# Attention inside a feed-forward kernel: products with v moved directly behind the scores, into another PSUM bank

## The chip, the cores and the metric

One core of a Trainium2 chip. The metric is the device time of one execution in microseconds, the median of the runs. TensorE is called PE here, VectorE DVE, ScalarE ACT, GpSimd POOL and SyncE SP.

## The reference

Windowed attention with eight memory keys for each head, followed by an RMS norm and a gated feed-forward layer, all in float32:

```python
for c in range(S // 32):                       # S = 768, chunks of 32 queries
    k_full = concat([mem_k, k[c0 - 16:c1 + 8]])  # 8 memory keys, 16 left, 32 own, 8 right
    a = softmax(q_c @ k_full.T / 8)
    out_c = a @ v_full
x = out as (4 * 768, 8 * 64)                   # tokens by heads * head_dim = 512
xn = x / sqrt(mean(x * x) + 1e-6) * rms_g
y = (silu(xn @ w_gate) * (xn @ w_val)) @ w_out  # d_ff = 1536
```

## The kernel before

**Blocks.** The 3072 tokens are eight blocks of 384. The feed-forward layer walks over them. Blocks 0 and 1 come first, in an order written out by hand (ORDER). Then come the segments of blocks 0, 2 and 3: for each of up to twelve slices f of d_ff, `moe_in` computes the gate `pg` (12 matmuls of 384 columns, three for each product because each float32 operand is held as a high and a low part), a second `moe_in` the value `pv` (12 more), and `moe_out` (L529) adds the product of the slice before into `po` (9 matmuls of 512 columns). Blocks 4 to 7 come last, two at a time, with products of combined operands (`whole`, `products`, L1001, and `out_products`, L1084).

**Late attention.** The attention of blocks 2 to 7 is not computed ahead: it is cut into steps, and a generator, `late_steps`, yields after each. It works on pairs of head units; n counts the pairs. One turn of the generator takes the pair `old`, whose softmax is done, through these steps: 'p' transposes the softmax of both units on PE (`stage_p`, L282, six transposes into two banks) and lets ACT copy them out (`stage_c`, L286, recorded at L181); 's' computes the scores of the next pair `cur` (`stage_s2`, L219), their maxima and differences on DVE and the exponentials on ACT (L247); 'o' multiplies the copies with v (`stage_o2`, L313), copies the result into x (`late_r`, L324), squares it on ACT (L327) and adds the squares on DVE (L329). After every second pair the norm follows: `late_n` splits the sum of squares and adds it over the partitions on PE (`ssum`, L341).

`stage_o2` writes the even chunks (`oe`) and the odd ones (`oo`) into two PSUM banks. `oe` takes one of the three rotating banks, and `oo`, where `own` is false (blocks 2 to 5), the bank of tag "v", which `pv` uses:

```python
stage_o2(old, None if own else "v")
```

The first unit's transposes use the gate's bank in these turns (`stage_p(u, None if i or own else "g")`). Each of these banks has a single buffer, so a new user waits for the last reader of the one before.

**Where the steps stand.** A table, VISITS, says which steps run in which gap of which segment. Gap 2n lies behind the gate of the n-th slice, 2n + 1 behind its value, and 2n + 1.5 behind the `moe_out` that follows. At 5: 'ps', 5.5: 'o' the transposes and scores run behind the value, then come the nine matmuls of `moe_out`, then the products with v, then the next slice's gate. The steps for blocks 6 and 7 (n from 9 on, `own` true) stand in a second table, SUPER, between the products of `whole(2)`.

**What sets the order.** From the segments on, PE runs in the order of the program (`on_pe`). The order on DVE, ACT, POOL and SP is made by a planner that goes by priorities; `tc.high_priority()` puts steps ahead, and `tc.issue_after(i)` puts an instruction behind another on its engine. Between the visits, DVE and ACT also compute sums of weights for the last blocks (`keep`, L838 to L851, and `sums_o`, L866 to L875), in amounts that tables give for each gap; each is issued behind the last DVE and ACT instructions traced so far. At n = 9 the step 'o' runs behind product 10 of the second pair of `whole(2)`; the add that takes a bank's result there (`add`, L977) is what frees the bank for the next product that uses it.

Of the kernel before, what the change touches and what calls it, by code (L numbers as in the profile page):

```python
# [14 lines left out]
ALU = mybir.AluOpType  # L15
# [24 lines left out]
YMAX = 0x1DFE / 0x1000 * 2.0 ** -96  # L40


VISITS = {0: {1: 's', 5: 'ps', 5.5: 'o', 7: 'ps', 7.5: 'o', 9: 'n', 10: 'n', 11: 'n'}, 2: {5: 'ps', 5.5: 'o', 17: 'ps', 17.5: 'o', 19: 'n', 20: 'nn'}, 3: {3: 'ps', 3.5: 'o', 7: 'ps', 7.5: 'o', 9: 'n', 9.5: 'n', 10: 'n', 11: 'ps', 11.5: 'o', 15: 'ps', 15.5: 'o', 17.5: 'n', 18: 'n', 19: 'n'}}
PAIRS = ((1, 2), (3, 4), (5, 6), (7, 8), (0, 9), (10, 11))
NR = 30

# [40 lines left out]
def tile_kernel(ctx: ExitStack, tc: tile.TileContext, q, k, v, w_gate, w_val, w_out, rms_g, out, out_t):  # L87
    nc = tc.nc
# [6 lines left out]
    ps = {"a": ps_cm.enter_context(tc.tile_pool(name="psa", bufs=3, space=PSUM))}  # L95
# [30 lines left out]
    def on_pe(ins):  # L126
        if pinned:
            tc.keep_in_program_order(ins)

    def psum_a(name):  # L130
        return ps["a"].tile([P, 512], F32, name=name, tag="at")

    def psum_m(tag, name):
        return psm.tile([P, 512], F32, name=name, tag=tag)
# [7 lines left out]
    late, late_cm = {}, {}  # L142
# [13 lines left out]
    def load_qk(u):  # L156
        d = st.setdefault(u, {})
        if u < NE:
            d["q"] = early.tile([P, HT], F32, name=f"q{u}", tag=f"q{u % 6}")
            t = early.tile([P, KN], F32, name=f"k{u}", tag=f"k{u % 6}")  # L160
            nc.sync.dma_start(out=d["q"], in_=q[u])
        else:

            t = late["kv", u % 2][:, 0:KN]
            d["q"] = late["q", u % 2]
            nc.sync.dma_start(out=d["q"], in_=q[u])
        d["k"] = t.rearrange("p (j k) -> p j k", j=NJ)
        nc.sync.dma_start(out=t, in_=k[u])

    def load_v(u):  # L170
        t = early.tile([P, VN], F32, name=f"vw{u}", tag=f"v{u % 6}") if u < NE else late["kv", u % 2][:, KN:]
        st.setdefault(u, {})["v"] = t.rearrange("p (j h d) -> p j h d", j=NJ, h=2)
        nc.sync.dma_start(out=t, in_=v[u])
# [33 lines left out]
    def stage_s2(pair):  # L207

        for u in pair:
            st[u]["s"] = psum_a(f"s{u}")  # L210
        for i in range(NT):
            for cp in range(2):
                for par in range(2):
                    c, o = 4 * i + 2 * par + cp, (2 * i + cp) * KC
                    for u in pair:
                        d = st[u]
                        for e in range(2):
                            r, a = slice(64 * e, 64 * e + 64), 64 * par + CH * (e ^ u % 2)
                            on_pe(nc.tensor.matmul(d["s"][a:a + CH, o:o + KC], lhsT=d["q"][r, c * CH:c * CH + CH],  # L219
                                                   rhs=d["k"][r, c // 2, 40 * cp:40 * cp + KC], start=True, stop=True))  # L220

    def stage_m(u):
        stage_ma(u)
        stage_mb(u)
# [20 lines left out]
    def stage_e(u):  # L245
        pe = st[u]["p"]
        nc.scalar.activation(pe, pe, AF.Exp, scale=0.125)  # L247

    def stage_d(u):
        stage_da(u)  # L250
        stage_db(u)
# [25 lines left out]
    def stage_p(u, tag=None):  # L277
        d = st[u]
        t = psum_m(tag, f"pT{u}") if tag else psum_a(f"pT{u}")
        pe = d["p"].rearrange("p j k -> p (j k)")  # L280
        for i in range(NT):
            on_pe(nc.tensor.transpose(out=t[:, i * P:(i + 1) * P], in_=pe[:, i * P:(i + 1) * P], identity=ident))  # L282
        d["t"] = t

    def stage_c(u):
        copy("a", late["pt", u % 2], st[u]["t"][:, 0:HT])  # L286
# [17 lines left out]
    def stage_o2(pair, tag):  # L304

        st["o2"] = o2 = [psum_a(f"oe{pair[0]}"), psum_m(tag, f"oo{pair[0]}") if tag else psum_a(f"oo{pair[0]}")]
        for j in range(NJ):
            for n, u in enumerate(pair):
                pt = late["pt", u % 2].rearrange("p (j e q) -> p j e q", j=NJ, e=2)
                for cp in range(2):  # L310
                    r, o = slice(64 * cp, 64 * cp + 64), (NJ * n + j) * CH
                    for hh in range(2):
                        on_pe(nc.tensor.matmul(o2[cp][64 * hh:64 * hh + 64, o:o + CH], lhsT=st[u]["v"][r, j, hh],  # L313
                                               rhs=pt[r, j, hh ^ u % 2], start=True, stop=True))

    def late_r(pair, x):

        g = units[pair[0]][2]
        o2 = st["o2"]
        for u in pair:  # L320
            st.pop(u)
        xc = x[g // 2].rearrange("p g (j c q) -> p g j c q", c=2, q=CH)
        for cp in (1, 0):
            nc.scalar.copy(xc[:, :, :, cp], o2[cp][:, 0:HT].rearrange("p (g j q) -> p g j q", g=2, q=CH))  # L324
        for i in range(g, g + 2):
            s = obuf(f"sq{i}")[:, 0:HT]
            nc.scalar.activation(s, x[i // 2][:, i % 2], AF.Square)  # L327
            if i:
                nc.vector.tensor_tensor(out=s, in0=s, in1=late["ss"], op=ALU.add)  # L329
            late["ss"] = s  # L330

    def late_n(x, parts=1):

# [198 lines left out]
    def obuf(name):  # L532
        return p3.tile([P, DM], F32, name=name, tag="stg")
# [30 lines left out]
    def last_of(eng):  # L564
        return next(i for i in reversed(nc.cur_bb.bb.instructions) if i.engine == eng.engine)
# [3 lines left out]
    def late_steps():  # L569


        pairs = [(u, u + 1) for u in range(NE, len(units), 2)]
        for n in range(len(pairs) + 1):
            old = pairs[n - 1] if n else ()
            cur = pairs[n] if n < len(pairs) else ()
            new = pairs[n + 1] if n + 1 < len(pairs) else ()
            own = bool(old) and old[0] >= 3 * 2 * NG
            if old and old[0] % NG == 0:
                if old[0] // NG in (5, 7):
                    late_x["x"] = [p1.tile([P, 2, HT], F32, name="x1", tag="wy"),  # L580
                                   late["tmp"][:, 0:2 * HT].rearrange("p (g t) -> p g t", g=2)]
                else:
                    t = p1.tile([P, NKT, HT], F32, name="xT", tag="x")
                    late_x["x"] = [t[:, 0:2], t[:, 2:4]]
                late_x[old[0] // NG] = late_x["x"]
            x = late_x.get("x")
            if old:
                with tc.high_priority():
                    for i, u in enumerate(old):
                        stage_p(u, None if i or own else "g")  # L590
                    for u in old:
                        stage_c(u)
                yield "p"
            if cur:
                with tc.high_priority():
                    stage_s2(cur)
                    for u in cur:
                        stage_m(u)
                    for u in cur:
                        stage_e(u)  # L600
            for u in new:
                load_qk(u)
            if old:
                if cur:
                    yield "s"
                with tc.high_priority():
                    stage_o2(old, None if own else "v")
                    late_r(old, x)
            norm = late_n(x, 1 if cur else 2) if n and n % 2 == 0 else ()
            behind = ExitStack()  # L610
            if norm:
                with tc.high_priority():
                    next(norm)
                behind.enter_context(tc.issue_after(last_of(nc.vector)))
            if own and norm and cur:
                for u in cur:
                    load_v(u)
                yield "o"
                next(norm)
                yield "n"  # L620
                with tc.high_priority():
                    for u in cur:
                        stage_d(u)
                yield "d"
            else:
                with tc.high_priority(), behind:
                    for u in cur:
                        stage_d(u)
                for u in cur if n else ():
                    load_v(u)  # L630
                yield "o" if old else "s"
            for _ in norm:
                yield "n"
# [79 lines left out]
    def tok_o(n):  # L713
# [15 lines left out]
        g=tok_in("g"), v=tok_in("v"), p=tok_q("g"), q=tok_q("v"),  # L729
# [427 lines left out]
    for blk, fs in segments:  # L1157
# [3 lines left out]
        def visit(gap):  # L1161
# [3 lines left out]
            sums_out()  # L1165
            for c in VISITS[blk].get(gap, ""):
                if next(todo) != c:
                    raise AssertionError(gap)
            keep(SUMS_AT[blk].get(gap, 0), summing)
        for n, f in enumerate(fs):  # L1170
            g = moe_in("g", f, xs)
# [132 lines left out]
```

## Time and profile before

| | us |
|---|---|
| median of 3 runs (652.34 to 655.0) | 652.45 |
| the profiled execution | 652.04 |
| its span, first to last instruction | 650.2 |
| PE busy | 638.2 |
| DVE busy | 489.4 |
| ACT busy | 366.2 |

The profile is of one execution. Busy time of PE counts each matmul from its start to a modelled end, and neighbours overlap, so that the distance from one start to the next is what a matmul costs in a run of them.

### The profile page before, as it was taken

How to read it: one execution, taken by the hardware profiler on the slowest of the kernel's cores; microseconds unless marked ns; L12 is line 12 of the kernel's file. 1: busy time of each engine (PE TensorE's matmuls, PEld its weight loads, DVE VectorE, ACT ScalarE, POOL GpSimd, SP SyncE). 2: the span in 40 equal slices, each digit the busy share in tenths (PEclk: the TensorE clock that was granted, in tenths of full speed). 3: DMA queues.
4: the chain of work that ended last, by engine and by line, in shares of the span. 5: the costliest groups of instructions: out<-in, count | busy, mean ns of one | idle time of the engine just before them, and what ended most of it. 6: DMA issues, size and time to landing. Idle time of an engine off the chain costs nothing.

```text
span 650.2 us, 15459 instructions
## 1 busy us (share of the span) xinstructions
PE 638.2 (98%) x6110; PEld 603.9 (93%) x6110; DVE 489.4 (75%) x999; ACT 366.2 (56%) x691; POOL 13.8 (2%) x19
## 2 busy tenths in 40 slices
PE   6999999999999999999999999999999999999997
PEld 4789999999899999999999999999999999999997
DVE  6999899768698888876888865567679854544864
ACT  4998877744545546465565454555566443333463
POOL 0200000000000000000000000000000000000000
PEclk7999999999999999999999999999999999999999
DMA  8737544269797887265459998887878988887711
GB/s 322 295 131 258 191 162 162 111 221 322 222 383 284 302 303 266 79 208 204 134 168 368 356 314 289 268 285 223 264 224 275 302 275 253 255 252 253 251 36 73
DMA packets 94006, 155.14 MB, mean 239 GB/s; under 512 B 8048, under 2 KB 47344, under 8 KB 93936
## 3 DMA queue, kind: packets, MB, share of 16 engines
q1 hardware_dynamic: 91920, 150.93, 69.2%
q10 hardware_dynamic: 2016, 3.25, 1.4%
q8 instruction: 48, 0.79, 0.5%
q14 instruction: 22, 0.18, 0.1%
HBM read 114.03 MB, written 40.11 MB: 237 GB/s over the span
## 4 chain that ended last, share of the span: by engine, by line
PE 94%; DMA 2%; ACT 2%; DVE 1%; issue 0%; SPq 0%
PE po L529 16%; PE pg L473 16%; PE pv L473 15%; PE mga L1001 8%; PE pa L1084 8%; PE mva L1001 8%; PE pe L1084 4%; PE mge L1001 4%; PE mve L1001 4%; PE oe L313 2%; PE s L219 2%; PE pc L1084 2%; PE mvc L1001 2%; PE mgc L1001 2%; PE pT L282 1%; DMA ws<-in_moe_w_val_dram 1%
## 5 line engine op out<-in xcount | busy, mean ns | idle before, releaser
L473 PE MATMUL pg<-xh,wh_g 128*128 128x384 f32 x192 | 65.9, 343 | 0.0
L473 PE MATMUL pv<-xh,wh_v 128*128 128x384 f32 x192 | 64.9, 338 | 0.5 <-ACT xT L324 0.5
L473 PE MATMUL pg<-xh,wl_g 128*128 128x384 f32 x192 | 64.6, 337 | 0.0
L473 PE MATMUL pg<-xl,wh_g 128*128 128x384 f32 x192 | 64.6, 336 | 0.0
L473 PE MATMUL pv<-xh,wl_v 128*128 128x384 f32 x192 | 64.3, 335 | 0.0
L473 PE MATMUL pv<-xl,wh_v 128*128 128x384 f32 x192 | 64.2, 334 | 0.0
L1001 PE MATMUL mga<-x,r 128*128 128x384 f32 x288 | 58.0, 335 | 0.0
L1001 PE MATMUL mva<-x,r 128*128 128x384 f32 x288 | 57.7, 334 | 0.0
L529 PE MATMUL po<-wh_o,hh 128*128 128x512 f32 x141 | 55.9, 396 | 0.0
L529 PE MATMUL po<-wl_o,hh 128*128 128x512 f32 x141 | 55.6, 394 | 0.0
L529 PE MATMUL po<-wh_o,hl 128*128 128x512 f32 x141 | 55.6, 394 | 0.0
L1052 ACT CAST hho<-h 128x384 fp32r<-128x384 f32 x72 | 37.0, 514 | 32.7 <-PE pa L1084 19.0
L1001 PEld LDWEIGHTS mva<-x,r 128*128 128x128 f32 x288 | 50.6, 188 | 0.0
L1001 PEld LDWEIGHTS mga<-x,r 128*128 128x128 f32 x288 | 50.5, 188 | 0.1
L1084 PE MATMUL pa<-hho,r 128*128 128x384 f32 x192 | 50.3, 335 | 0.0
L1053 DVE TENSOR_TENSOR hlo<-h,hho 128x384 fp32r<-128x384 f32 x72 | 39.3, 555 | 13.3 <-ACT hho L1052 12.4
L181 ACT CAST hh<-t 128x384 fp32r<-128x384 f32 x45 | 23.2, 516 | 44.1 <-PE po L529 20.3
L473 PEld LDWEIGHTS pg<-xh,wh_g 128*128 128x128 f32 x192 | 36.1, 188 | 1.8
L473 PEld LDWEIGHTS pv<-xh,wh_v 128*128 128x128 f32 x192 | 36.0, 188 | 1.7 <-ACT xT L324 0.9
L473 PEld LDWEIGHTS pg<-xl,wh_g 128*128 128x128 f32 x192 | 36.1, 188 | 1.4 <-DVE xl L676 0.2
L473 PEld LDWEIGHTS pv<-xl,wh_v 128*128 128x128 f32 x192 | 36.0, 188 | 0.3
L473 PEld LDWEIGHTS pg<-xh,wl_g 128*128 128x128 f32 x192 | 36.0, 188 | 0.0
(195 smaller groups left out, 1561.3 us busy)
## 6 DMA issues: line engine op xcount, KB each, us to landing
r<-kg SPq DMA_DIRECT2D x84, 256.0 KB, 3.8
r<-kv SPq DMA_DIRECT2D x84, 256.0 KB, 3.6
r<-ko SPq DMA_DIRECT2D x84, 256.0 KB, 3.2
kv<-in_v_dram SPq DMA_DIRECT2D x24, 384.0 KB, 4.4
kv<-in_k_dram SPq DMA_DIRECT2D x24, 312.0 KB, 4.4
q<-in_q_dram SPq DMA_DIRECT2D x20, 192.0 KB, 4.2
ws<-in_moe_w_gate_dram SPq DMA_DIRECT2D x6, 512.0 KB, 3.7
ws<-in_moe_w_val_dram SPq DMA_DIRECT2D x6, 512.0 KB, 4.6
```

The costliest lines, as they stand in the source:

```text
L181: return nc.scalar.copy(out, in_)
L219: on_pe(nc.tensor.matmul(d["s"][a:a + CH, o:o + KC], lhsT=d["q"][r, c * CH:c * CH + CH], rhs=d["k"][r, c // 2, 40 * cp:40 * cp + KC], star ...
L282: on_pe(nc.tensor.transpose(out=t[:, i * P:(i + 1) * P], in_=pe[:, i * P:(i + 1) * P], identity=ident))
L313: on_pe(nc.tensor.matmul(o2[cp][64 * hh:64 * hh + 64, o:o + CH], lhsT=st[u]["v"][r, j, hh], rhs=pt[r, j, hh ^ u % 2], start=True, stop=True))
L473: on_pe(nc.tensor.matmul(ps[:, 0:HT], lhsT=weight(a, n, f, kt), rhs=xs[c][:, kt], start=kt == first and i == 0, stop=kt == last and i == 2))
L529: on_pe(nc.tensor.matmul(po[i], lhsT=h[a][:, i * P:(i + 1) * P], rhs=weight(c, "o", f), start=f == first and n == 0, stop=f == end and n = ...
L1001: on_pe(nc.tensor.matmul(bank[w, b], lhsT=r[:, a, kt], rhs=x[:, c, kt], start=bool(first) and kt == 0 and i == 0, stop=kt == 1 and i == 2, ...
L1052: nc.scalar.copy(hh, x)
L1053: nc.vector.tensor_tensor(out=hl, in0=x, in1=hh.bitcast(F32), op=ALU.subtract)
L1084: on_pe(nc.tensor.matmul(bank[c][i], lhsT=w[u][:, x, i * P:(i + 1) * P], rhs=uhl[u][y], start=p == 0 and n == 0 and m in (1, 2, 5), stop=p ...
```

## The change

The eight visits in blocks 0, 2 and 3 run 'pso' in one gap, behind the value and ahead of `moe_out`; the gaps 2n + 1.5 are empty after it. In these turns the odd products go into the bank of tag "g". For the odd n with `own` true (9 and 11), the second add of squares is not issued in `late_r`: it is held and issued at the start of the next turn, ahead of its transposes.

```diff
-VISITS = {0: {1: 's', 5: 'ps', 5.5: 'o', 7: 'ps', 7.5: 'o', 9: 'n', ...
+VISITS = {0: {1: 's', 5: 'pso', 7: 'pso', 9: 'n', ...
...
-    def late_r(pair, x):
+    def late_add(s):
+        nc.vector.tensor_tensor(out=s, in0=s, in1=late["ss"], op=ALU.add)
+        late["ss"] = s
+
+    def late_r(pair, x, hold=False):
...
             nc.scalar.activation(s, x[i // 2][:, i % 2], AF.Square)
-            if i:
-                nc.vector.tensor_tensor(out=s, in0=s, in1=late["ss"], op=ALU.add)
-            late["ss"] = s
+            if not i:
+                late["ss"] = s
+            elif hold:
+                late["held"] = s
+            else:
+                late_add(s)
...
             if old:
                 with tc.high_priority():
+                    if "held" in late:
+                        late_add(late.pop("held"))
                     for i, u in enumerate(old):
                         stage_p(u, None if i or own else "g")
...
-                    stage_o2(old, None if own else "v")
-                    late_r(old, x)
+                    stage_o2(old, None if own else "g")
+                    late_r(old, x, own and n % 2 == 1)
```

In segment 2 the gaps 5 and 17 are changed in this way, in segment 3 the gaps 3, 7, 11 and 15.

## Rows read from the trace of the kernel before

**Rows 1.** Page: busy time and instructions by engine, and the chain that ended last.

```profile
PE 638.2 (98%) x6110; PEld 603.9 (93%) x6110; DVE 489.4 (75%) x999; ACT 366.2 (56%) x691; POOL 13.8 (2%) x19
...
PE 94%; DMA 2%; ACT 2%; DVE 1%; issue 0%; SPq 0%
```

**Rows 2.** Busy time by stretch: bounds, us, then each engine, granted clock, DMA.

```profile
150.00:328.00 178.00, 177.32 (x2184) 163.20 (x2183) 147.36 (x331) 94.67 (x193) 2.43 (x2) 1.00 0.72 244
```

**Rows 3.** PE's timeline in one visit: start, us, line, tiles, shape, count.

```profile
169.89 0.23 PE L219 MATMUL s<-kv,qp 64*32 64x64 f32 x2
170.05 0.50 PE L529 MATMUL po<-wh_o,hh 128*128 128x512 f32 x1
...
171.31 0.39 PE L529 MATMUL po<-wh_o,hl 128*128 128x512 f32 x1
...
171.99 0.39 PE L529 MATMUL po<-wh_o,hl 128*128 128x512 f32 x1
172.31 0.25 PE L313 MATMUL oe<-pt,kv 64*64 64x32 f32 x2
...
173.69 0.23 PE L313 MATMUL oo<-kv,kv 64*64 64x32 f32 x2
173.84 0.45 PE L473 MATMUL pg<-xh,wh_g 128*128 128x384 f32 x1
174.13 0.34 PE L473 MATMUL pg<-xl,wh_g 128*128 128x384 f32 x1
174.30 0.35 PE L473 MATMUL pg<-xh,wl_g 128*128 128x384 f32 x1
```

**Rows 4.** PE's timeline after the visit at 157 us; idle time and releaser in brackets.

```profile
165.14 0.34 PE L473 MATMUL pg<-xh,wl_g 128*128 128x384 f32 x1
166.01 0.44 PE L473 MATMUL pv<-xh,wh_v 128*128 128x384 f32 x1 [0.53 <-ACT xT L324]
166.29 0.34 PE L473 MATMUL pv<-xl,wh_v 128*128 128x384 f32 x1
```

**Rows 5.** ACT's timeline, same stretch.

```profile
165.49 0.47 ACT L324 COPY xT<-oo 128x384 f32<-128x384 f32 x1
```

**Rows 6.** PE's timeline in `whole(2)`, behind the step 'o' of n = 9.

```profile
399.83 1.20 PE L1001 MATMUL mva<-x,r 128*128 128x384 f32 x6
401.72 1.32 PE L1001 MATMUL mve<-x,r 128*128 128x384 f32 x6 [0.69 <-DVE e L977]
```

**Rows 7.** DVE's timeline, same stretch.

```profile
400.64 0.56 DVE L329 TENSOR_TENSOR sq<-sq,sq 128x384 f32<-128x384 f32 x1 [2.83 <-ACT sq L327]
401.12 0.55 DVE L977 TENSOR_TENSOR e<-mve,e 128x384 f32<-128x384 f32 x1
```

**Rows 8.** PE's timeline at the norm's column sums.

```profile
261.01 0.34 PE L341 MATMUL ssum<-sh,one 128*128 128x384 f32 x1
261.49 0.44 PE L341 MATMUL ssum<-sl,one 128*128 128x384 f32 x1
```

**Rows 9.** ACT's timeline in the visit of rows 3.

```profile
169.10 0.49 ACT L181 COPY kv<-pT 128x384 f32<-128x384 f32 x1
171.64 0.53 ACT L247 ACTIVATE pe<-pe 128x384 f32<-128x384 f32 x1 [2.06 <-DVE pe L242]
...
173.95 0.48 ACT L324 COPY xT<-oe 128x384 f32<-128x384 f32 x1 [0.82 <-PE oo L313]
174.32 0.48 ACT L324 COPY xT<-oo 128x384 f32<-128x384 f32 x1
```

**Rows 10.** PE's timeline at the scores' end, visits at 251 and 319 us.

```profile
252.75 0.23 PE L219 MATMUL s<-kv,qp 64*32 64x64 f32 x2
...
321.24 0.23 PE L219 MATMUL s<-kv,qp 64*32 64x64 f32 x2
```

**Rows 11.** ACT's timeline in these two visits.

```profile
252.55 0.47 ACT L181 COPY kv<-pT 128x384 f32<-128x384 f32 x1
...
325.37 0.94 ACT L247 ACTIVATE pe<-pe 128x384 f32<-128x384 f32 x2
```

More of the change, by code (lines that the diff above doesn't have):

```diff
@@ L40 @@
 YMAX = 0x1DFE / 0x1000 * 2.0 ** -96
-VISITS = {0: {1: 's', 5: 'ps', 5.5: 'o', 7: 'ps', 7.5: 'o', 9: 'n', 10: 'n', 11: 'n'}, 2: {5: 'ps', 5.5: 'o', 17: 'ps', 17.5: 'o', 19: 'n', 20: 'nn'}, 3: {3: 'ps', 3.5: 'o', 7: 'ps', 7.5: 'o', 9: 'n', 9.5: 'n', 10: 'n', 11: 'ps', 11.5: 'o', 15: 'ps', 15.5: 'o', 17.5: 'n', 18: 'n', 19: 'n'}}
+VISITS = {0: {1: 's', 5: 'pso', 7: 'pso', 9: 'n', 10: 'n', 11: 'n'}, 2: {5: 'pso', 17: 'pso', 19: 'n', 20: 'nn'}, 3: {3: 'pso', 7: 'pso', 9: 'n', 9.5: 'n', 10: 'n', 11: 'pso', 15: 'pso', 17.5: 'n', 18: 'n', 19: 'n'}}
 PAIRS = ((1, 2), (3, 4), (5, 6), (7, 8), (0, 9), (10, 11))
```

## The prediction

> **What bounds the kernel.** I read the page first. PE is busy for 638.2 of 650.2 us, and the chain that ended last is PE for 94% of the span [rows 1]. So a change is worth what it takes out of PE's stream of instructions, or puts in; DVE (75%) and ACT (56%) count where they hold PE up. I then asked for the busy time of the stretch in which most of the moved visits lie [rows 2]. [...] There is no half-clock time to win back and only 0.68 us of plain idle time. The rest of what can be gained lies in the spacing of the starts, which busy time does not show, since a matmul's record is about twice as long as its step (0.39 us against 0.23 us).
>
> So the third view is PE's timeline of one visit, read start to start [rows 3]. In a run of 128x512 matmuls the step is 0.23 us (three steps from 171.31 to 171.99), in a run of 128x384 it is 0.17 us (174.13 to 174.30). The steps at a change of matmul shape are longer. From the scores (64*32) to `po` it is 0.16 us (169.89 to 170.05), from `po` to the products with v (64*64) 0.32 us, from these to the gate 0.15 us, and after the gate's first matmul 0.29 us in place of 0.17. All eight visits up to the fourth block repeat these four steps within 0.02 us. Last come the real stalls. There are three: 0.53 us of idle time before `pv` at 166.01 us [rows 4], 0.69 us before `mve` at 401.72 us [rows 6], and a step of 0.48 us in place of 0.17 to the second `ssum` at 261.49 us [rows 8].
>
> **Part 1: products with v behind the scores, eight visits.** No matmul is added or removed; the 48 products only stand before the nine `po` matmuls of L529, no longer behind them. Before, PE pays two excursions into small shapes: transposes and scores, back to `po`, products, back to the gate. What the second one costs beside its own products is (0.32 - 0.23) + 0.15 + (0.29 - 0.17) = 0.36 us [rows 3]. After, products lead straight into `po` with the steps that the scores have now, and `po` goes into the gate at the plain 0.23 us. The new step is from scores to products, 64*32 to 64*64, which the trace of before does not show. If it cost nothing, a visit would gain 0.36 us; the transition from scores to another shape that is there is 0.16 us. The longest that could apply is the excess of a step into small shapes together with one out of them, 0.09 + 0.16 = 0.25 us. I take 0.15, the nearest row. A visit gains 0.21 us and eight gain 1.7 us; the ends are 0.9 us and 2.9 us.
>
> [...]
>
> The new order has a condition. The products need both transposed copies that ACT makes (L286), and now only the scores lie in between. In the visit at 168 us the second copy starts at 169.10 and lasts 0.49 us [rows 9], so it ends at 169.59; the scores' last matmuls start at 169.89 [rows 3] and the products would start at 170.04: 0.45 us of cover. Where the planner has a weight cast between the two copies, as at 252 us, the second copy ends at 252.55 + 0.47 = 253.02 [rows 11], while the products would be due at 252.75 + 0.15 = 252.90 [rows 10]. That costs about 0.1 us of waiting and 0.1 us for the long step after a wait: 0.2 us lost, in one visit.
>
> **Part 2: the odd products in the gate's bank.** Before, `oo` sits in the value's bank, and `pv` must wait until ACT has copied it out. In the visit at 157 us this is late: ACT has weight casts (L846) that wait for DVE queued ahead and copies `oo` only at 165.49 us [rows 5]. `pv` starts 0.87 us after `pg`'s last matmul where 0.17 is plain, and the matmul after it takes 0.28 us [rows 4]: 0.70 + 0.11 = 0.8 us. The wait goes with the bank. What is late next is the gate: its first matmul now waits for the copy of `oo`. Its due time, counted from the scores' last start, is 0.15 + 1.38 (products, 172.31 to 173.69) + 0.15 + 2.17 (`po`, 1.94 from 170.05 to 171.99 and a step of 0.23) = 3.85 us [rows 3]. `oo` is complete at 0.15 + 1.38 + 0.23 = 1.8 us. If ACT first does both exponentials, which begin at 171.64 - 169.89 = 1.75 us and follow each other at 0.5 us, then the two copies at 0.37 us (173.95 to 174.32) with 0.48 us for the last [rows 9], it is done at 1.75 + 1.0 + 0.37 + 0.48 = 3.6 us. That is 0.25 us ahead. The cast of `hh` cannot come in between: it waits for the same nine `po` matmuls to finish reading the old `hh`, and they now stand behind the products. The weight casts are queued behind `hh`. So I cost the bank at nothing, with thin cover. The visit at 319 us has none if the exponentials go first: they begin at 325.37 [rows 11], 4.1 us behind the scores [rows 10]. There the copies must be queued ahead of them.
>
> The sums of squares and the norm of a visit follow the copies and move forward with them, by up to 2 us against PE. The `ssum` stall at 261.49 us, which waits for that chain (0.31 us [rows 8] and 0.1 us in the next step as in rows 4, 0.4 us), ends if the chain gains 0.3 us. But DVE's weight sums of that visit are now queued behind the whole visit. I count half, 0.2 us. Loads keep their number and their order within SP's queue; those of v are issued as soon as the products have read the old v, which is earlier, and no load is on the path in these stretches [rows 2].
>
> **Part 3: the held sum of squares.** At 400.64 us DVE starts the add of L329, for which it has been waiting idle 2.83 us on ACT's squares; behind it stands the add that frees the bank `mve`, which starts at 401.12 [rows 7], and PE waits for this one until 401.72 [rows 6]. PE's idle 0.69 us, with the 0.17 us that the stall of rows 4 lost beyond its idle time and the 0.11 us of the step after it, is 0.97 us. With the add put off to the next visit, DVE is free when `mve` is complete, which is about 0.17 us after PE goes on to `mva` at 399.83 [rows 6]. The freeing add then ends at about 400.0 + 0.55 = 400.55, and PE would need the bank at 401.72 - 0.86 = 400.86 at the earliest: no wait is left. The second held add (the pair at 456 us) stands before no stall. Both adds cost their 0.56 us later, in DVE's idle time.
>
> **The sum**, against the profiled execution of 652.04 us (span 650.2 and 1.8 around it; the median of the runs is 652.45, 0.4 above): -1.7 - 0.8 - 0.97 - 0.2 + 0.2 = -3.5 us, 648.5 us profiled, 649.0 us for the median.
>
> **Rivals.** *The held add is not put off.* It is free to be scheduled as soon as the squares are there, and nothing but its place in the program holds it back. The planner did let `stage_d` overtake that add in other visits, so it goes by readiness, and it may put the add where it was. Then 0.97 us stays: 650.0 us. *The gate waits in a few visits.* At 319 us exponentials first means `oo` copied at about 4.1 + 0.94 + 0.37 + 0.48 = 5.9 us, which is 2.0 us late; with one exponential first 0.4 us less. One such visit: 650.6 to 651.0 us. *The other side: the gate waits in all eight.* If the planner queues the copies behind the cast of `hh`, they begin at about 3.9 us and end at 4.8, 0.95 us late, and 0.1 us more for the step: eight times 1.05 is 8.4 us, 657.4 us. It decides from 0.4 us a visit on (no gain) and makes a slower kernel from 0.85 us. Against it speaks that `hh` depends on matmuls behind the products. *The order of small matmuls gives nothing*: products straight after scores cost 0.36 us more than either alone; then 652.45 - 1.8 = 650.7 us.
>
> **How the numbers follow.** 0.5% of 652.45 is 3.26 us, about what a measurement can tell from no change, so the bound lies at 649.2, close to my sum. The forecast has 0.52 (648.0 to 649.8 by its own terms), the add not put off 0.23, a gate wait in one or a few visits 0.10, no gain from the merged order 0.06, the gate late everywhere 0.09. The forecast is below 649.2 in 0.41 of its 0.52; add 0.03 for the second with a free step. So faster 0.44, within 0.5% 0.47, slower 0.09. The lower end is everything with a free step, 652.45 - 2.9 - 0.8 - 0.97 - 0.4 = 647.4, which I cut to 647.9; the upper end takes in the one-visit wait, 651.3.
>
> **What would show it.** Right: scores to products about 0.15 us, `po` to gate 0.23 us, no idle time before `pv` in the visit at 157 us or before the gate in any of the eight; L329 at n = 9 behind the add of `mve`, and no wait near 400 us. Wrong: a PE wait on L324 before a gate matmul, a wait on L286 before the products in more than one visit, L329 still at 400 us, or a new DVE wait before `po` from the weight sums that are pushed back.

## The result, and the profile after

The changed kernel takes 660.86 us (median of four runs, 658.62 to 662.13) beside 652.84 us for the kernel before beside it: a ratio of 1.0108, 95% interval 1.0090 to 1.0127. The forecast was 649.0 us with a range of 647.9 to 651.3; the kernel got slower instead. The profiled execution took 660.25 us with a span of 658.1.

The lines of the changed kernel are numbered 4 to 9 higher (one more in experiments 5 and 6): L473 is now L480 (`pg` and `pv`), L529 is L536 (`po`), L324 is L328 (the copies of `oe` and `oo`), L977 is L986, L1001 is L1010, L838 to L851 are L847 to L860. The add of squares, L329, is now L317.

**How much of it is the change.** Up to the first visit both programs are the same, yet its transposes start at 160.39 us here and at 157.46 before. So I split each span at that point. From there to the end the kernel before takes 650.25 - 157.46 = 492.8 us and the changed one 658.13 - 160.39 = 497.7 us (spans to the hundredth): 4.95 us are lost in the changed part, and 2.9 us ahead of it (more on the start below).

**The page of the profile**, the lines that answer to [rows 1], and the queue that brings instructions:

```profile
PE 642.7 (98%) x6110; PEld 608.5 (92%) x6110; DVE 489.4 (74%) x999; ACT 365.4 (56%) x691; POOL 13.1 (2%) x19
...
q8 instruction: 48, 0.79, 0.5%
...
PE 88%; DVE 5%; DMA 3%; ACT 2%; issue 1%; SPq 0%; DVEq 0%; ACTq 0%
```

The counts of instructions are those of before; PE's share of the chain has fallen from 94% to 88%, so PE now waits. For what, the view of PE's waits from 150 to 412 us says (us in total, times, longest):

```profile
PE pg L480 <- ACT x L328: 1.4, 1, 1.4
PE oe L313 <- ACT kv L181: 1.3, 1, 1.3
PE oo L313 <- issue: 0.9, 1, 0.9
PE oe L313 <- issue: 0.8, 1, 0.8
PE mve L1010 <- DVE e L986: 0.7, 1, 0.7
PE po L536 <- ACT hlast L1220: 0.2, 1, 0.2
```

The wait of `pv` for the copy of `oo` [rows 4] is gone, the wait of `mve` [rows 6] is as it was, and five others are new.

**The order itself.** PE's timeline in the first visit, which has no wait (columns as in [rows 3]):

```profile
162.07 0.23 PE L219 MATMUL s<-kv,qp 64*32 64x64 f32 x2
162.23 0.25 PE L313 MATMUL oe<-pt,kv 64*64 64x32 f32 x2
...
163.61 0.23 PE L313 MATMUL oo<-kv,kv 64*64 64x32 f32 x2
163.77 0.50 PE L536 MATMUL po<-wh_o,hh 128*128 128x512 f32 x1
...
165.72 0.39 PE L536 MATMUL po<-wh_o,hl 128*128 128x512 f32 x1
165.95 0.33 PE L480 MATMUL pg<-xh,wh_g 128*128 128x384 f32 x1
166.12 0.34 PE L480 MATMUL pg<-xl,wh_g 128*128 128x384 f32 x1
```

Scores to products is 0.15 us, products to `po` 0.16, `po` to gate 0.23, and the gate's second matmul follows after a plain 0.17. From the first transpose to the first gate matmul a visit takes 165.95 - 160.39 = 5.56 us; before, it took 173.84 [rows 3] less its start at 168.20, 5.64 us. With the long step inside the gate that is gone (0.29 to 0.17 us) a visit gains 0.19 us, where 0.21 was forecast.

**The two stops.** PE's timeline in the second visit:

```profile
172.59 0.28 PE L313 MATMUL oe<-kv,kv 64*64 64x32 f32 x4
173.74 0.25 PE L313 MATMUL oo<-kv,kv 64*64 64x32 f32 x2 [0.87 <-issue]
```

In the middle of the products, between two matmuls that follow each other in 0.01 to 0.06 us elsewhere, PE stands still for 0.87 us, and no semaphore ends it: the view writes "issue". The same happens in the fifth visit at 295.46 us (0.82 us). What was under way is on queue q8. In the view of the DMA queues from 170.90 to 171.10 us (40 slices) one transfer begins at 170.98:

```profile
DMA  0000000000000009000000000000000000000000
...
q8 instruction: 1, 0.02, 42.3%
```

The 48 transfers of 0.79 MB on the page are 16,384 bytes each; what one of them brings is called a block of instructions from here on. By the trace's records this one lasts 1.35 us, to 172.33, and PE goes on 2.76 us after it began. Before, the transfer for the same place in PE's stream of instructions begins at 169.25 us (the same view from 169.20 to 169.40), and PE comes to that place only 3.6 us later, at 172.82:

```profile
DMA  0500000000900000001000000000000000000000
...
q8 instruction: 1, 0.02, 29.9%
```

**The copy.** In the visit at 254 us PE waits 1.30 us for the second copy of `pT`. ACT's timeline, DVE's, and PE's:

```profile
253.79 1.32 ACT L855 CAST kh<-ks 128x256 fp32r<-128x256 f32 x3 [1.18 <-DVE ks L850]
255.02 0.47 ACT L181 COPY pt<-pT 128x384 f32<-128x384 f32 x1
256.39 0.40 ACT L855 CAST kh<-ks 128x256 fp32r<-128x256 f32 x1 [0.89 <-DVE ks L850]
256.70 0.47 ACT L181 COPY kv<-pT 128x384 f32<-128x384 f32 x1
```

```profile
255.33 0.69 DVE L847 TENSOR_TENSOR qp<-wh_v,wl_v 128x512 f32<-128x512 f32 x1 [0.65 <-DMA kv<-qp]
```

```profile
257.23 0.25 PE L313 MATMUL oe<-pt,kv 64*64 64x32 f32 x2 [1.30 <-ACT kv L181]
...
259.22 0.63 PE L536 MATMUL po<-wl_o,hh 128*128 128x512 f32 x1
259.64 0.63 PE L536 MATMUL po<-wh_o,hl 128*128 128x512 f32 x1
```

This is the weight cast between the copies that the forecast had seen [rows 11], but it is itself late: DVE's sum stands behind another that waits for a DMA. Then comes a second price. The steps of `po` are 0.42 us instead of 0.23, and the windows show why (columns as in [rows 2]):

```profile
257.00:258.80 1.80, 1.57 (x97) 1.53 (x97) 1.68 (x4) 1.77 (x3) 0.00 (x0) 1.00 0.64 222
258.80:262.40 3.60, 3.60 (x13) 2.83 (x10) 1.12 (x2) 2.71 (x7) 0.00 (x0) 0.53 1.01 311
262.40:266.00 3.60, 3.60 (x23) 3.56 (x21) 3.44 (x13) 1.84 (x3) 0.00 (x0) 1.00 0.62 238
```

Behind the pause the granted clock falls to 0.50 (the view from 259.10 to 262.20 us) and comes back to 1.00. From `po` to the gate it is 3.75 us instead of 2.18: 1.57 us lost.

**The gate.** In the visit at 325 us (319 us before) ACT has both exponentials ahead of the copies, the case named in the forecast; PE's gate waits 1.38 us, its step is 1.77 us in place of 0.23:

```profile
330.81 0.99 ACT L247 ACTIVATE pe<-pe 128x384 f32<-128x384 f32 x2 [2.63 <-DVE pe L242]
331.70 0.46 ACT L328 COPY x<-oe 128x384 f32<-128x384 f32 x1
332.06 0.48 ACT L328 COPY x<-oo 128x384 f32<-128x384 f32 x1
```

```profile
330.82 0.39 PE L536 MATMUL po<-wh_o,hl 128*128 128x512 f32 x1
332.59 0.45 PE L480 MATMUL pg<-xh,wh_g 128*128 128x384 f32 x1 [1.38 <-ACT x L328]
```

**The held add** stands where it stood in [rows 7], with the same idle time:

```profile
408.52 0.56 DVE L317 TENSOR_TENSOR sq<-sq,sq 128x384 f32<-128x384 f32 x1 [2.83 <-ACT sq L331]
408.99 0.55 DVE L986 TENSOR_TENSOR e<-mve,e 128x384 f32<-128x384 f32 x1
```

**Account of the changed part**, us, start to start on PE:

| | forecast | profiled |
|---|---|---|
| merged order, eight visits | -1.7 | -1.5 |
| `pv` behind `oo` (157 us) | -0.8 | -0.8 |
| held add, `mve` | -0.97 | 0 |
| `ssum` (261 us; step of `ssum` to `po` 0.76, now 0.35) | -0.2 | -0.4 |
| wait for the copy (251 us) | +0.2 | +1.4 |
| half clock behind that wait | 0 | +1.6 |
| two stops in the products | 0 | +2.2 |
| gate behind the copies (319 us) | 0 | +1.6 |
| `hlast`, the high part of the last slice's product (374 us after), cast on ACT behind DVE's `t` | 0 | +0.7 |
| sum | -3.5 (with rounding) | +4.8; measured +4.95 |

### The profile page after: what moved, and what is told of

Its sections match the earlier page's. It is cut to its first block, busy times and chain, and to the rows that moved or that the text cites. A ratio compares the mean times of both kernels' runs of the same rounds, so it can differ in the third digit from the quotient of the medians.

```text
span 658.1 us, 15463 instructions
## 1 busy us (share of the span) xinstructions
PE 642.7 (98%) x6110; PEld 608.5 (92%) x6110; DVE 489.4 (74%) x999; ACT 365.4 (56%) x691; POOL 13.1 (2%) x19
## 4 chain that ended last, share of the span: by engine, by line
PE 88%; DVE 5%; DMA 3%; ACT 2%; issue 1%; SPq 0%; DVEq 0%; ACTq 0%
PE pg L480 14%; PE pv L480 13%; PE po L536 13%; PE mga L1010 8%; PE pa L1093 8%; PE mva L1010 7%; PE mge L1010 4%; PE pe L1093 4%; PE mve L1010 4%; PE pc L1093 2%; PE mvc L1010 2%; PE mgc L1010 2%; PE s L219 2%; PE pT L282 2%; PE oe L313 2%; PE o L299 1%
## 5 line engine op out<-in xcount | busy, mean ns | idle before, releaser
L480 PE MATMUL pg<-xh,wh_g 128*128 128x384 f32 x192 | 65.1, 339 | 1.4 <-ACT x L328 1.4
L480 PE MATMUL pv<-xh,wh_v 128*128 128x384 f32 x192 | 64.8, 337 | 0.0
L480 PE MATMUL pg<-xl,wh_g 128*128 128x384 f32 x192 | 64.6, 337 | 0.0
L480 PE MATMUL pg<-xh,wl_g 128*128 128x384 f32 x192 | 64.6, 337 | 0.0
L480 PE MATMUL pv<-xh,wl_v 128*128 128x384 f32 x192 | 64.3, 335 | 0.0
L480 PE MATMUL pv<-xl,wh_v 128*128 128x384 f32 x192 | 64.2, 334 | 0.0
L1010 PE MATMUL mga<-x,r 128*128 128x384 f32 x288 | 58.0, 335 | 0.0
L1010 PE MATMUL mva<-x,r 128*128 128x384 f32 x288 | 57.7, 334 | 0.0
L536 PE MATMUL po<-wh_o,hh 128*128 128x512 f32 x141 | 56.6, 401 | 0.0
L536 PE MATMUL po<-wh_o,hl 128*128 128x512 f32 x141 | 56.3, 399 | 0.0
L536 PE MATMUL po<-wl_o,hh 128*128 128x512 f32 x141 | 56.3, 399 | 0.0
L1010 PEld LDWEIGHTS mva<-x,r 128*128 128x128 f32 x288 | 50.6, 188 | 0.0
L1010 PEld LDWEIGHTS mga<-x,r 128*128 128x128 f32 x288 | 50.5, 188 | 0.1
L480 PEld LDWEIGHTS pg<-xh,wh_g 128*128 128x128 f32 x192 | 36.2, 188 | 3.5 <-ACT x L328 1.8
L480 PEld LDWEIGHTS pg<-xl,wh_g 128*128 128x128 f32 x192 | 36.1, 188 | 1.8 <-DVE xl L685 0.2
L480 PEld LDWEIGHTS pv<-xh,wh_v 128*128 128x128 f32 x192 | 36.0, 188 | 0.8 <-DVE t L504 0.3
L480 PEld LDWEIGHTS pv<-xl,wh_v 128*128 128x128 f32 x192 | 36.1, 188 | 0.3
L480 PEld LDWEIGHTS pv<-xh,wl_v 128*128 128x128 f32 x192 | 36.0, 188 | 0.0
```

The source lines that it names most:

```text
L480: on_pe(nc.tensor.matmul(ps[:, 0:HT], lhsT=weight(a, n, f, kt), rhs=xs[c][:, kt], start=kt == first and i == 0, stop=kt == last and i == 2))
L536: on_pe(nc.tensor.matmul(po[i], lhsT=h[a][:, i * P:(i + 1) * P], rhs=weight(c, "o", f), start=f == first and n == 0, stop=f == end and n = ...
L1010: on_pe(nc.tensor.matmul(bank[w, b], lhsT=r[:, a, kt], rhs=x[:, c, kt], start=bool(first) and kt == 0 and i == 0, stop=kt == 1 and i == 2, ...
```

## The experiments

Three questions: what the stops are; what the bank and the copy cost by themselves; and what the start and the held add are.

**1. Moving the program along.** Matmuls of zeros are put into the start of the changed kernel, where PE waits for loads, some 150 us ahead of the visits. 16 of them are 32 matmul records and 32 weight loads, 64 instructions (the page counts 6142 of each in place of 6110).

```diff
-U0 U1 U2 Z U3 S0 U4 M0 ...
+U0 U1 U2 Z U3 W32 S0 U4 M0 ...     # first kernel, 128 instructions
+U0 U1 U2 Z U3 W16 S0 U4 M0 ...     # second kernel, 64 instructions
```

> [...] Theory A (PE runs out of instructions: a visit now runs 397 small instructions in a row, and where two block borders fall into it the second block is not there yet): the stops of about 1.1 us inside the products of the visits at 170 and 292 us go away, because only one border falls into these now, and stops of 0.5 to 1.5 us appear in up to six others (160, 213, 254, 309, 325, 343 us), whose second border comes to lie inside the products: 3 to 5 us slower than the changed kernel. Theory B (the stops belong to these two visits' data: their loads of v, a bank, a semaphore): both stops stay where they are, at the same matmul, and the time is that of the changed kernel within 1 us.

> The same with 16 matmuls, 64 instructions. Theory A: the first border of each visit then lies 146 or more instructions behind its start, no visit holds two borders, and no stop is left inside any products: about 2.1 us faster than the changed kernel. Theory B: both stops stay, time unchanged.

With 128 instructions: 672.12 us, ratio 1.0287 (1.0241 to 1.0332). With 64: 654.75 us, ratio 1.0020 (1.0010 to 1.0030), 6 us less than the changed kernel. PE's waits of the first, up to 365 us, and of the second, up to 412 us (one of 0.2 us left out):

```profile
PE oo L313 <- issue: 8.2, 5, 2.4
PE po L536 <- issue: 1.2, 1, 1.2
PE oe L313 <- issue: 1.2, 1, 1.2
```

```profile
PE pg L480 <- ACT x L328: 1.4, 1, 1.4
PE oe L313 <- ACT kv L181: 0.7, 2, 0.4
PE mve L1010 <- DVE e L986: 0.7, 1, 0.7
PE po L536 <- issue: 0.3, 1, 0.3
...
```

The same matmuls in the same order on PE, shifted by 128 instructions, stop in six other visits (in the products of the first, third, fourth, sixth, seventh and eighth; and in `po` of the fifth), no longer in the second; shifted by 64, in no products at all (0.3 us are left in `po` behind the eighth visit's). So a stop belongs to a place in the instruction stream and not to an operand. The places are a fixed distance apart. The windows from one stop to another, first in the changed kernel, then between the first three stops of the 128-instruction kernel and one further pair, count PE's matmuls and weight loads:

```profile
173.20:295.00 121.80, 119.59 (x1148) 111.08 (x1147) 101.01 (x214) 61.77 (x128) 2.43 (x2) 0.99 0.73 253
```

```profile
167.50:221.00 53.50, 51.58 (x637) 48.05 (x637) 43.55 (x95) 28.07 (x58) 1.39 (x1) 1.00 0.87 297
221.00:265.50 44.50, 42.59 (x382) 39.47 (x383) 36.14 (x77) 20.54 (x46) 0.00 (x0) 0.96 0.75 261
...
321.50:339.20 17.70, 16.41 (x255) 15.22 (x254) 13.25 (x31) 9.65 (x18) 0.00 (x0) 1.00 0.42 133
```

2295, 1274, 765 and 509 instructions are 9, 5, 3 and 2 times 254.5 to 255: always a whole number of blocks (of instructions here, not of tokens). The transfers on q8 agree: in the changed kernel 48 of them, of 16,384 bytes each, for PE's 12,220 counted instructions, 254.6 each.

The time that a block takes comes from the records. In the eleven stops of the two profiles of the changed kernel (the second is in part 4) and of the first experiment, PE goes on 2.3 to 2.8 us after the block's transfer began, of which the transfer itself takes 0.9 to 1.5 us. Small matmuls use up a block faster: in the second visit 132 matmuls and 125 weight loads, about one block, start in the 1.74 us from 170.96 to 172.70. Transposes, scores and products are now one run of nearly 400 instructions in 3.4 us. In all eleven stops the transfer began only as PE passed the border before or behind it (4 to 254 counted instructions behind), and PE was at the next border before the block could be used. Two borders in one run do not stop it every time: in the changed kernel's third visit they lie about 7 and 262 instructions behind the run's start, but there the transfer began at 210.83 us, 1.9 us ahead of the visit, and PE goes through. What decides when a transfer begins is not shown. Before, nine `po` matmuls of 0.23 us each stood between the scores and the products, and no visit stopped.

Both times moved further than the theory had said, 11 us up for 3 to 5 and 6 us down for 2.1. Behind the first visit the profiles have 505.9 us with 128 instructions and 494.3 with 64, beside 497.7 and 496.4 in the two profiles of the changed kernel: 8.2 to 9.5 us more, and 2.1 to 3.4 us less. With 128 the stops are longer than expected (1.15 to 2.35 us idle), and three of them are followed by half clock. With 64 there is more to the gain than the stops: no half clock comes, and the wait for the copy is two of 0.4 us in place of one of 1.3 (in that execution DVE does not wait for the DMA there). The rest lies ahead of the first visit (163.33 and 157.94 us) or in runs without a profile.

**2. The odd products back in the bank of the value**, all else as changed:

```diff
-                    stage_o2(old, None if own else "g")
+                    stage_o2(old, None if own else "v")
```

> The changed kernel with the odd products in the value's bank again, the merged order kept; the order of instructions on every engine is the same as in the changed kernel. If the wait of the gate at 332 us (1.55 us, and 0.1 us behind it) comes from the bank alone, it goes, and no wait appears before any value, because the value's matmuls come 2.1 us after the gate's: 1.6 us faster than the changed kernel. If the late copy matters through something else, a wait of that size appears elsewhere in that visit.

657.66 us, ratio 1.0057 (1.0036 to 1.0077). No gate waits any more, and neither does a `pv`: with the merged order the copies lie early enough for the bank of the value in all eight visits, the first one included. The stops and the wait for the copy with its half clock are there as before. So the move of the bank was not needed to take away the wait in [rows 4]; the earlier products did it alone, and the gate's bank only brought the wait, 1.6 us with the step behind it.

**3. The weight sums of one gap shortened**, so that ACT has both copies of the visit at 254 us next to each other:

```diff
-KEEP = {..., 2: {..., 14: 1792, 22: 1024, ...
+KEEP = {..., 2: {..., 14: 1280, 18: 512, 22: 1024, ...
```

> The changed kernel with 512 columns of the weight sums moved from gap 14 to gap 18 of segment 2, so that no weight cast stands between the two copies of the visit at 254 us. If that cast, which waits for DVE and through it for a store, holds up the second copy and with it the products (1.37 us), and the half clock that follows (1.57 us over nine matmuls) comes from that pause, both go: 2.9 us faster than the changed kernel, granted clock 1.00 throughout the stretch. If the products there waited for something else, the pause stays at about 1.3 us; if the half clock has another cause, it stays.

657.84 us, ratio 1.0059 (1.0038 to 1.0081). The wait and the half clock at that place are gone. The median is 3.0 us lower, as expected, but the profiled execution, the slowest of the four, does not show that gain behind the first visit (498.0 us beside 497.7): in it the pause in the fifth visit is followed by half clock instead, which costs 1.6 us there, the gate waits 0.3 us longer, and the moved sums make `hh`, which `po` reads, late at 279 us (0.4 us). So the expectation of full clock throughout the stretch failed.

**4. The start, and each kernel once more.** The kernel before with the 16 matmuls of zeros alone, and both kernels unchanged in a further profile:

```diff
-U0 U1 U2 Z U3 S0 U4 M0 ...
+U0 U1 U2 Z U3 W16 S0 U4 M0 ...     # in the kernel before
```

> The kernel before with the 16 matmuls of zeros (64 PE instructions) at the start that e2 had, and nothing else. Theory (in e2 they help only because they move the borders of the instruction blocks out of the merged visits; before, a visit has about 200 PE instructions ahead of its nine large matmuls and no stop): the time of before within 0.2%, and no stop of over 0.5 us without a releaser in any of the eight visits. Rival (the 16 matmuls are worth something at the start, by an earlier full clock or an earlier load): faster than before by about what e2 gained over after, 6 us, or at least by 1.5 us.

> The kernel before, unchanged, profiled once more. Theory (the 2.9 us that the kernel after lost ahead of the first visit are a difference between executions, since both programs are the same there and one other profile of it, with the held add alone, begins the first po 1.3 us later): the first po starts 0 to 3 us after the 43.3 us of the first profile, and from there to the end all steps repeat within 0.2 us. Rival (the start belongs to the program): the first po within 0.2 us of 43.3 us.

> The kernel after, unchanged, profiled once more. Theory: the stops in the products of the visits at 170 and 292 us, the wait for the copy at 257 us and the wait of the gate at 332 us all stand again at the same matmuls, with 0.8 to 1.8 us each; what differs is the start (0 to 3 us) and which pause is followed by a stretch of 3.4 us at half clock. Rival (the stops are events of one execution): at least one of the two stops is missing or stands at other matmuls. If the start belongs to the program: the first po within 0.2 us of 46.2 us.

The matmuls of zeros do nothing for the kernel before: 652.81 us, ratio 0.9997 (0.9987 to 1.0006), no stop. So they are worth nothing by themselves, and what they gave the changed kernel depends on its order. The first visit and the rest, by execution:

| | first visit, us | from there to the end, us |
|---|---|---|
| before, first profile | 157.46 | 492.8 |
| before, second profile (653.53 us) | 158.90 | 492.9 |
| after, first profile | 160.39 | 497.7 |
| after, second profile (657.51 us) | 159.04 | 496.4 |

The start moves by 1.4 us between executions of one program, and the first profile of before was early. So half of the 2.9 us or more is no part of the change. That nothing of it is, these profiles do not show: all four of the merged order without zeros start at 159.04 to 160.39 us, the three of the order before without zeros at 157.46 to 158.90, although the order on PE is the same up to there. In the second profile of after the two stops stand at the same matmuls (172.20 and 292.70 us), the copy's wait and the gate's are there, and no half clock follows any of them: the changed part takes 1.3 us less.

**5. The held add by itself**, in the kernel before, tied behind the last DVE instruction of the turn before:

```diff
+                    if "held" in late:
+                        with tc.issue_after(last_of(nc.vector)):
+                            late_add(late.pop("held"))
```

> The kernel before with the held add alone, now tied by issue_after to the last DVE instruction of the turn before, so that on DVE it stands behind the adds that free the banks. Theory (in the kernel after, holding had no effect because the planner put the add back where its operands were ready; the stall before mve hangs on that add alone): the idle time before mve near 401.7 us goes (0.69 us idle, 0.97 us with the steps around it) and the time falls by 0.7 to 1.0 us, a ratio of about 0.9985. Rival (another wait takes its place, since the freeing add is late for a reason of its own): DVE's instruction that frees the bank still starts after 400.9 us, PE still waits 0.5 us or more there, and the time is that of before within 0.1%. Beside it: the start of this execution, up to the first visit, shows how far the start of the same program moves from execution to execution (0 to 3 us, if the 2.9 us that the kernel after lost there are no part of the change).

652.64 us, ratio 0.9988 (0.9978 to 0.9998). DVE's timeline and PE's:

```profile
401.41 0.56 DVE L987 TENSOR_TENSOR e<-mve,e 128x384 f32<-128x384 f32 x1 [2.29 <-PE mve L1011]
...
406.08 0.55 DVE L317 TENSOR_TENSOR sq<-sq,sq 128x384 f32<-128x384 f32 x1
```

```profile
401.14 1.21 PE L1011 MATMUL mva<-x,r 128*128 128x384 f32 x6
402.19 1.22 PE L1011 MATMUL mve<-x,r 128*128 128x384 f32 x6
```

The add now stands 4.7 us behind the one that frees the bank, PE has no wait before `mve`, and from the first visit to the end it is 491.8 us: 1.0 us less than before, where 0.97 was worked out. That the planner goes by readiness shows in the start's control too: with the 16 matmuls of zeros in the kernel before, the planner itself put the add behind `mve`, and the stall was gone without any edit to it.

**6. All four losses taken away:** the bank of the value, 12 matmuls of zeros (48 instructions, with which no run of a visit holds two borders), shorter weight sums in two gaps, and the tied add.

```diff
-KEEP = {..., 2: {..., 14: 1792, 22: 1024, ...}, 3: {..., 2: 1536, 5: 2048, ..., 12: 512}}
+KEEP = {..., 2: {..., 14: 1280, 18: 512, 22: 1024, ...}, 3: {..., 2: 1024, 5: 2560, ..., 12: 512}}   # first version
+KEEP = {..., 2: {..., 14: 1280, 22: 1024, ...}, 3: {..., 2: 1024, 5: 2560, ..., 12: 1024}}           # second version
-U0 U1 U2 Z U3 S0 U4 M0 ...
+U0 U1 U2 Z U3 W12 S0 U4 M0 ...
-                        late_add(late.pop("held"))
+                        with tc.issue_after(last_of(nc.vector)):
+                            late_add(late.pop("held"))
-                    stage_o2(old, None if own else "g")
+                    stage_o2(old, None if own else "v")
```

> The kernel after with all four found losses taken away: the odd products in the bank of the value again, 12 matmuls of zeros (48 PE instructions) at the start, so that no block border falls into the scores or products of a visit, the weight sums of two gaps shortened so that both copies stand next to each other on ACT in all eight visits, and the held add tied behind the add that frees the bank. Theory (the order itself is worth 0.19 us a visit, and stops of the instruction supply, the copies and the gate bank gave it back): no stop over 0.4 us in any visit but the old wait before pv in the first one, granted clock 1.00 there, and 2 to 3.5 us less than before, a ratio of 0.995 to 0.997. Rival (the merged order as such costs, the stops only move): the time of before or longer, with new idle time in visits where the kernel after has none.

> The kernel with all four losses taken away, but the 512 columns of weight sums that it had moved right behind the fourth visit (where the norm then came late, and po waited at 276 us, 0.8 us with the steps around it) moved to the third segment instead. Theory (that wait comes from the moved sums alone): no wait over 0.3 us in po near 276 us, and 0.8 us less than that version, a ratio to before of about 0.9955. Rival (DVE and ACT are so full there that sums moved anywhere make something else late): another wait of 0.4 us or more appears and the ratio stays at 0.997.

The first version takes 651.19 us beside 653.5, ratio 0.9969 (0.9956 to 0.9981); the second 651.56 beside 653.67, the same ratio (0.9958 to 0.9979). PE's waits from 150 to 412 us in the one and in the other:

```profile
PE po L536 <- ACT hh L785: 0.4, 1, 0.4
PE po L536 <- ACT hlast L1221: 0.2, 1, 0.2
```

```profile
PE pg L480 <- ACT t L495: 0.6, 1, 0.6
PE po L536 <- ACT hlast L1221: 0.2, 1, 0.2
```

No visit stops, the granted clock is 1.00 from the first visit to the last, and the first version takes 491.1 us from the first visit to the end, 1.7 less than before. The sums that were taken out of one gap made something else late in both places where I put them, 0.8 us with the steps around it in each version: there the rival of the last experiment was right, and the two together suggest that DVE and ACT have little room left in this stretch.

## Why the prediction was wrong

**Right: the price of the order.** 0.19 us a visit for 0.21, with the step from scores to products at 0.15 us as taken from the nearest row; it is there in every visit of the last kernels. So the step is paid, and not free. The stall before `pv` is gone (-0.8), and the one at `ssum` (-0.4, forecast -0.2). But "the wait goes with the bank" named a cause that was not needed: experiment 2 has the old bank and no wait, since the copies now come earlier.

**The step that failed: what a visit needs besides its operands.** "No matmul is added or removed; the 48 products only stand before the nine `po` matmuls" looked at the steps between shapes and at semaphores alone. The nine large matmuls had been the time in which PE's next block of instructions arrived (in the visit at 168 us its transfer began 3.6 us before PE came to it), and no row that I had read showed that, since before nothing waited for it. The prediction had no term for it, and the two stops cost 2.2 us. Experiments 1 and 4 show that they come from the place of the borders: a shift of 64 instructions takes the stops out of the products of the changed kernel (2.1 to 3.4 us less behind the first visit, with a shorter wait for the copy in it), one of 128 puts them into six other visits, and the kernel before, shifted by 64, has none and gains nothing. The stops are the largest single term that was missing, but not the whole miss of 8.3 us: the copy, the half clock behind it, the gate and the held add below make up most of the rest.

**The copy was mis-sized.** 0.2 us were forecast for one visit, at the right visit and with the right cast between the copies; 1.3 us of idle time came, 1.4 us with the step. I had taken the start of the second copy from before [rows 11], as if the cast ahead of it were always ready. It waits for DVE, and DVE for a DMA. The half clock behind the pause, 1.57 us, was in no term at all.

**The bank was costed at nothing, and one visit paid.** The condition was stated ("there the copies must be queued ahead of them") and not met; the rival with 2.0 us in this visit was right in mechanism, and measured 1.6 us. The rival that made a slower kernel, the gate late in all eight visits, did not come: no other gate waits. Experiment 2 shows more: the bank did not need to move.

**The held add** went as its rival said: the planner put it where its operands are ready. Experiment 5 shows that the working of the 0.97 us was sound, and that only the tie was missing.

**What stays open.** The changed part accounts for 3.6 to 4.95 us in the two profiles, and their starts lie 1.5 us later on average than the two of before, about what one program shows between executions. The medians of the first comparison differ by 8.0 us, so that some 2 to 3 us lie in runs without a profile, where I can't place them. Half clock behind more than one pause, at 1.6 us each, would do it, but that is argued only. Whether a part of the later start goes with the program is open too. The late `hlast` (0.7 us) is in all profiles of the merged order but those of experiment 1 (none with 128 instructions, some 0.15 us with 64), and was not tried by itself.

## What to carry to other kernels

Before joining two runs of small matmuls, count the instructions of the joint run, weight loads included, and its duration: where it passes more than one block (some 255 counted instructions here) in less than the 2.3 to 2.8 us that a block took here, it can stop, and whether it did hung here on how many instructions stood ahead in the program: products or `po` stopped in two visits as it was, in seven with 128 instructions more, and in one `po` alone, for 0.3 us, with 64. Such a kernel's time says little about the edit until the alignment has been varied, and a part of what a change seems to cost may be a border that it met (here 2.2 of the 4.95 us of the changed part). An instruction that is meant to be late needs a tie to what it is to follow; a later place in the program alone is no order where a planner goes by readiness.

## What was not expected of the hardware

The stops of the instruction supply showed in no wait of a semaphore, only as idle time with the releaser "issue" and one transfer of 16,384 bytes on q8; the longest was 2.35 us.

Pauses of PE of 1 us or more cost clock in some of these executions and not in others. Of 22 pauses of 0.67 us or more in the visits of these profiles, six (idle 1.00, 1.15, 1.30, 1.44, 1.48 and 2.35 us) were followed by a stretch at the lower clock, which cost 1.3 to 1.6 us where `po` stood in it; others as long (1.36, 1.41, 1.49, 1.68 and 1.75 us) were not, and the same pause in two executions of one program did both. What decides it was not settled.
